# A filter's second layer on TensorE in quarter tiles, one step ahead, with one product moved from PSUM to SBUF

## Chip, core and metric

The kernel runs on one core of one Trainium2 chip. The metric is the device time of one execution in microseconds (us), the median of several runs. On the core, TensorE (PE in the profile, its weight loads PEld) multiplies matrices into PSUM; VectorE (DVE), ScalarE (ACT) and GpSimd (POOL) work element by element; SyncE (SP) issues most of the transfers. PSUM has eight banks of 512 float32 values in each of 128 partitions; SBUF is the large on-chip memory.

## The reference, cut to what matters

```python
def _attn_ref(x, v, pos_emb, w1, w2):            # x, v: 1 x 12480 x 128
    h_mlp = np.maximum(pos_emb @ w1, 0.0) @ w2   # filter: 64 features, second layer 64 -> 128
    h_filt = h_mlp * np.exp(-0.01 * pos)[:, None]
    Uf = np.fft.rfft(x * v, n=2 * S, axis=1)
    Hf = np.fft.rfft(h_filt, n=2 * S, axis=0)
    y = np.fft.irfft(Uf * Hf[None, :, :], n=2 * S, axis=1)[:, :S, :]
    return x * y
# then two mixture layers on the 12480 x 128 result:
#   g = relu(x @ w_in) ** 2;                x = g @ w_out
#   g = max(h, 0) + alpha * min(h, 0), h = x @ w_in2;   out = g @ w_out2
```

## The kernel before

The convolution is done with a Fourier transform of length 110 x 229, written as matrix products; it takes the first 313 us or so of the execution, the two dense layers the rest. The stages of the convolution follow each other: the filter's hidden layer (`z_stage`), its transform (`ar_stage`, `r_stage`), the signal's transform (`u_stage`), the product of both (`p_stage`), and the way back (`b_stage`, `y_stage`). The second layer of the filter, `w2`, is linear, so it is applied after the transform, inside `p_stage`: the transformed hidden layer lies in tiles `r` (three in SBUF, the others are fetched back from a spill in DRAM).

`p_stage(h, ...)` makes the product for one half h of the 128 channels, in 14 steps n (0 to 13 for h=0, 14 to 27 for h=1). A step covers 4 of the 56 frequencies of the length-110 transform. In each step:

- `filters(n, c)` (line 363) makes the filter's real (c=0) and imaginary (c=1) part on TensorE: four matmuls of 128 rows, 115 columns of weights and 128 moving columns for each c. The 128 rows are two frequencies of 64 features, and `w2_sb` is a block-diagonal matrix, half of it zeros, that keeps the two apart. Each goes to one of the two banks of `r_h`. A float32 matmul shows as two rows in the trace, so a step has 16 such rows.
- VectorE multiplies the signal's transform with each part (line 386): `T` gets one product, and the second goes to `wide`, a PSUM tile of two banks, or in the steps listed in `on_pool` to a second `T` tile in SBUF. In half 0 each product is two instructions (16 and 112 channels), in half 1 one.
- Two sums of 512 elements (line 396) turn the products into a complex one: on VectorE, from `T` and `wide`, or on GpSimd in the steps in `on_pool`.
- `finish` (line 357) adds and subtracts pairs of channels and writes the result over the signal's transform: on GpSimd, except in the very last step, where VectorE does it.

There are four `T` tiles, used in turn. What runs beside the two halves: half 0 runs together with `u_stage(1)`, the signal's transform for the other channels (lines 312 to 328 on TensorE, ScalarE and VectorE; lines 274 and 211 on GpSimd prepare its input); half 1 runs together with `b_stage(0)` (line 409 on TensorE, line 413 on ScalarE), which reads what half 0 has written. `b_stage(1)` reads what half 1 has written, so it starts when the last `finish` is done, and everything behind it follows. `run` takes turns between two generators, and each engine's queue is the order in which the program was written; nothing reorders it.

Names in the rows: `bank` and `pair` are PSUM banks, `G` and `R` hold the transforms of the two halves (and other things at other times), `w_sb` is the second layer's matrix, `w_buf` and `s_w`, `f_w`, `m_w` are buffers for decoding the dense layers' weights, which lie idle during `p_stage`.

```python
            for c, op in ((0, ALU.subtract), (1, ALU.add)):
                eng = nc.gpsimd if apart else nc.vector
                eng.tensor_tensor(out=A[:, :, c], in0=A[:, :, c], in1=B[:, :, 1 - c], op=op)
            finish(n, j, A)
```

Of the kernel before, what the change touches and what calls it, by code (L numbers as in the profile page):

```python
# [9 lines left out]
F32 = mybir.dt.float32  # L10
# [11 lines left out]
KA = HA + 1  # L22
# [36 lines left out]
def kernel(  # L59
# [18 lines left out]
    idft_o: bass.AP,  # L78
    out: bass.AP,
# [10 lines left out]
    six = [psum.tile([128, 512], F32, name=f"bank{i}") for i in range(6)]  # L90
    s_pair = ctx.enter_context(ExitStack())

    def last_two(name, *sizes):
        s_pair.close()
        pool = s_pair.enter_context(tc.tile_pool(name=name, bufs=1, space=PSUM))
        return [pool.tile([128, n], F32, name=f"{name}{i}") for i, n in enumerate(sizes)]

    banks = six + last_two("pair", 512, 512)
    r_any, r_six, r_a, r_b, r_h = Ring(banks), Ring(six), Ring(banks[0:2]), Ring(banks[2:5]), Ring(banks[5:8])
# [61 lines left out]
    def load_first(pool):  # L161
# [13 lines left out]
        nc.sync.dma_start(out=sig_sb, in_=sign)  # L175
        nc.sync.dma_start(out=dfa, in_=dft_a)
        load(3)
# [35 lines left out]
    def ar_stage():  # L213
# [7 lines left out]
        for c in range(F // 4):  # L221
            f0 = 4 * c
            p = [bank(r_six, HB, 4, K2) for s in range(2)]
            for s in range(2):
                for j in range(4):
                    nc.tensor.matmul(p[s][:, j], lhsT=rv[:, f0 + j, s], rhs=dfa[:, s * K2:(s + 1) * K2])  # L226
# [118 lines left out]
    on_pool = {2, 6, 10, 15, 18, 21, 24}  # L345

    def p_stage(h, t_ring, r_ring):
# [20 lines left out]
        first = []  # L368
        if h:
            first += [filters(nj, c) for c in range(2)]  # L370
            yield
        for n in range(h * nj, (h + 1) * nj):
# [7 lines left out]
            B = t_ring() if apart else wide[:HB].rearrange("p (x c k) -> p x c k", k=4, c=2)  # L380
            A = t_ring()
            for c, out_c in enumerate((A, B)):
                H = first.pop(0) if first else filters(n, c)
                hv = H.rearrange("p d s q r -> p (d s) (q r)")
                for x0, m in parts(h):
# [3 lines left out]
                        in1=hv[:, x0:x0 + m].unsqueeze(2).to_broadcast([HB, m, 2, 4]),  # L389
# [108 lines left out]
    def split_w(s, f, m, t, hi, lo, tail):  # L498
        words = s.rearrange("p t k -> p (t k)").bitcast(I32).rearrange("p (n w) -> p w n", w=2)
# [30 lines left out]
    def weights(pool, n=2):  # L530
        s_ring = ring_of(pool, 3, [128, n, 128], I64, "s_w")
        rings = [ring_of(pool, 2, [128, n * 128], F32, t) for t in ("f_w", "m_w")] + [Ring([])]

        def go(todo):
# [217 lines left out]
    with tc.manual_schedule():  # L752
        wst = ctx.enter_context(tc.tile_pool(name="wst", bufs=1))
        decode = weights(wst)
# [8 lines left out]
        with ExitStack() as st:  # L763
            late = st.enter_context(tc.tile_pool(name="late", bufs=1, side="right"))
            w2_sb = late.tile([128, 2 * D], F32, name="w2_sb")
# [18 lines left out]
            (wide,) = last_two("wide", 1024)  # L784
            r_b.items, r_h.items, r_ab.items = six[2:4], six[4:6], six[0:4]
# [98 lines left out]
def _tables(cell):  # L884
# [9 lines left out]
    ic[0] *= 0.5  # L894
    dft_b = np.zeros((HB, 3, HX), f)
# [8 lines left out]
    return w[cell].astype(f), dft_a, dft_b, e.astype(f), np.stack([o, -o], 1).astype(f)  # L904
# [59 lines left out]
```

## Time and profile before

| what | before |
|---|---|
| median of 3 runs | 1384.12 us (1383.98 to 1384.48) |
| profiled execution, its own time | 1384.36 us |
| span of the profiled execution | 1382.6 us |
| busy: TensorE, VectorE, ScalarE, GpSimd | 1374.7, 1146.6, 984.4, 1029.3 us |
| granted TensorE clock, mean | 1.00 |

The profiled execution's own time is its span and 1.8 us around it. The share of TensorE over the whole span says little on one stage: the product stage lies between about 118 and 243 us, and there three engines have nearly the same load. So the rows are read by stretch: 118 to 195.1 us is half 0 of the product, 195.1 to 243.3 us half 1. A timeline row merges instructions of one kind that follow each other: start, length in us, engine, line, operation, tiles, shapes and count, and in brackets the idle time of the engine before it with what ended it. Matmul ends are modelled, so the distance from start to start is read, not the length.

### The profile page before, as it was taken

To read this page: it belongs to the slowest core of one execution; us is meant where nothing else is said; L and a number is where in the kernel's file an instruction comes from. 1 tells how busy PE (TensorE), PEld (TensorE's weight loads), DVE (VectorE), ACT (ScalarE), POOL (GpSimd) and SP (SyncE) were. 2 spreads that over 40 slices of the span, in tenths; PEclk is the share of its full clock that TensorE was granted. 3 is DMA by queue.
4 is the path that set the end of the run, shared out by engine and by line. 5 is a ranking of instruction groups with operands and counts; after the bars stand their busy time and mean duration, and the time that the engine had idled before them with its cause. 6 is when DMAs were issued, how large, how long until landed. Compare 5 with 4: busy or idle time off the path is not lost.

```text
span 1382.6 us, 23568 instructions
## 1 busy us (share of the span) xinstructions
PE 1374.7 (99%) x8036; PEld 1193.9 (86%) x8036; DVE 1146.6 (83%) x1806; ACT 984.4 (71%) x1863; POOL 1029.3 (74%) x857
## 2 busy tenths in 40 slices
PE   9999999999999999999999999999999999999998
PEld 9999999998888888888888888888888888888898
DVE  6888989867888888888888878888888878888888
ACT  4453333638887777877777787778777787778777
POOL 4955969577877777777777777777777777777777
PEclk9999999999999999999999999999999999999999
DMA  8666423574000000000000000000000000000000
GB/s 250 185 199 186 129 65 114 157 245 146 31 2 0 9 9 1 8 9 8 9 9 9 8 1 9 9 8 8 9 8 1 9 8 8 9 9 9 1 8 19
DMA packets 59020, 66.27 MB, mean 48 GB/s; under 512 B 6226, under 2 KB 48019, under 8 KB 58771
## 3 DMA queue, kind: packets, MB, share of 16 engines
q1 hardware_dynamic: 58490, 64.56, 15.2%
q8 instruction: 63, 1.03, 0.3%
q14 instruction: 58, 0.48, 0.1%
q10 hardware_dynamic: 409, 0.21, 0.1%
HBM read 47.83 MB, written 16.92 MB: 47 GB/s over the span
## 4 chain that ended last, share of the span: by engine, by line
PE 96%; DVE 2%; issue 1%; POOL 1%; ACT 0%; POOLq 0%; DVEq 0%; ACTq 0%
PE bank L637 19%; PE bank L638 19%; PE bank L639 19%; PE pair L638 6%; PE pair L639 6%; PE pair L637 6%; PE bank L409 3%; PE bank L466 3%; PE bank L363 3%; PE bank L286 2%; PE bank L226 2%; PE bank L312 2%; PE bank L299 1%; PE pair L245 1%; PE bank L191 1%
## 5 line engine op out<-in xcount | busy, mean ns | idle before, releaser
L690 POOL TENSOR_TENSOR g<-R,g 128x512 fp32r<-128x512 f32 (+1 forms) x601 | 779.6, 1314 | 257.9 <-ACT g L679 243.7
L672 DVE SCALAR_TENSOR_TENSOR R<-bank,e 128x512 f32<-128x512 f32 (+1 forms) x800 | 530.8, 674 | 137.0 <-POOL g L690 99.2
L679 ACT CAST g<-R 128x512 fp32r<-128x512 f32 (+1 forms) x800 | 469.6, 605 | 76.6 <-DVE R L672 69.2
L657 ACT ACTIVATE e<-bank 128x512 f32<-128x512 f32 (+1 forms) x400 | 234.9, 587 | 104.0 <-PE bank L639 101.3
L662 DVE TENSOR_SCALAR e<-bank,alpha 128x512 f32<-128x512 f32 (+1 forms) x266 | 195.2, 734 | 35.9 <-PE bank L639 34.6
L690 DVE TENSOR_TENSOR g<-R,g 128x512 fp32r<-128x512 f32 (+1 forms) x199 | 185.0, 930 | 0.0
L638 PE MATMUL pair<-g,w_o 128*128 128x512 f32 (+1 forms) x400 | 153.7, 384 | 0.4 <-POOL g L690 0.4
L637 PE MATMUL bank<-x,w_i 128*128 128x512 f32 (+1 forms) x400 | 153.8, 385 | 0.0
L637 PE MATMUL pair<-g,w_o 128*128 128x512 f32 (+1 forms) x400 | 153.7, 384 | 0.0
L638 PE MATMUL bank<-x,w_i 128*128 128x512 f32 (+1 forms) x400 | 153.6, 384 | 0.0
L639 PE MATMUL bank<-x,w_i 128*128 128x512 f32 (+1 forms) x400 | 153.5, 384 | 0.0
L639 PE MATMUL pair<-g,w_o 128*128 128x512 f32 (+1 forms) x400 | 153.5, 384 | 0.0
L637 PE MATMUL bank<-g,w_o0b 128*128 128x512 f32 (+1 forms) x350 | 134.4, 384 | 0.0
L638 PE MATMUL bank<-g,w_o0b 128*128 128x512 f32 (+1 forms) x350 | 134.4, 384 | 0.0
L639 PE MATMUL bank<-g,w_o0b 128*128 128x512 f32 (+1 forms) x350 | 134.3, 384 | 0.0
L659 ACT ACTIVATE e<-bank 128x512 f32<-128x512 f32 (+1 forms) x134 | 78.8, 588 | 34.1 <-PE bank L639 32.5
L660 ACT ACTIVATE e<-e,alpha 128x512 f32<-128x512 f32 (+1 forms) x134 | 95.5, 713 | 4.4
L637 PEld LDWEIGHTS bank<-x,w_i 128*128 128x128 f32 x400 | 75.1, 188 | 15.0 <-DVE R L672 0.9
L638 PEld LDWEIGHTS pair<-g,w_o 128*128 128x128 f32 x400 | 75.1, 188 | 14.7 <-POOL g L690 1.0
L639 PEld LDWEIGHTS bank<-x,w_i 128*128 128x128 f32 x400 | 75.1, 188 | 14.4
L639 PEld LDWEIGHTS pair<-g,w_o 128*128 128x128 f32 x400 | 75.1, 188 | 14.4
L638 PEld LDWEIGHTS bank<-x,w_i 128*128 128x128 f32 x400 | 75.3, 188 | 13.8
(138 smaller groups left out, 2531.9 us busy)
## 6 DMA issues: line engine op xcount, KB each, us to landing
r<-spill SPq DMA_DIRECT2D x22, 460.0 KB, 3.3
G<-in_xs_dram SPq DMA_DIRECT2D x32, 224.0 KB, 3.8
G<-in_vs_dram SPq DMA_DIRECT2D x32, 224.0 KB, 3.7
spill<-r SPq DMA_DIRECT2D x14, 460.0 KB, 3.0
out_dram<-R SPq DMA_DIRECT2D x23, 256.0 KB, 2.0
s_w<-in_moe_w_out_dram SPq DMA_DIRECT2D x16, 256.0 KB, 5.3
s_w<-in_moe_w_in_dram SPq DMA_DIRECT2D x16, 256.0 KB, 2.9
w_spill<-w_o SPq DMA_DIRECT2D x15, 256.0 KB, 4.2
```

Of the source, the lines that this page charges most:

```text
L363: nc.tensor.matmul(H[:, :, s, q], lhsT=r_t[p_order[n]][:, q, 2 * s + c], rhs=w2_sb[:, h * D:(h + 1) * D])
L409: nc.tensor.matmul(p[:, d], lhsT=U(h, 2 * (x0 + d) + e, 1)[:, 0], rhs=icosb if e == 0 else isinb)
L637: nc.tensor.matmul(p, lhsT=wl, rhs=xh, start=first, stop=False)
L638: nc.tensor.matmul(p, lhsT=wh, rhs=xl, start=False, stop=False)
L639: nc.tensor.matmul(p, lhsT=wh, rhs=xh, start=False, stop=last)
L657: nc.scalar.activation(out=r, in_=p, func=ACTF.Relu)
L659: nc.scalar.activation(out=r, in_=p, func=ACTF.Relu, scale=-1.0)
L660: nc.scalar.activation(out=r, in_=r, func=ACTF.Copy, scale=alpha[:, t:t + 1])
L662: nc.vector.tensor_scalar(out=r, in0=p, scalar1=0.0, scalar2=alpha[:, t:t + 1], op0=ALU.min, op1=ALU.mult)
L672: nc.vector.scalar_tensor_tensor(out=g, in0=p, scalar=0.0, in1=r, op0=ALU.max, op1=op)
L679: nc.scalar.copy(out=gh, in_=g)
L690: eng.tensor_tensor(out=gl, in0=g, in1=gh.bitcast(F32), op=ALU.subtract)
```

## The change

- `filters(n)` now makes both parts in one call, with 32 matmuls in place of 8. Each takes 64 rows (one frequency), 64 or 51 columns of weights, and 64 moving columns, so it uses one quarter of the array; the four quarters (two row groups, two column groups) come in turn. The two row groups write to different banks. `w2_sb` holds the 64 x 128 matrix twice, one below the other, without zeros.
- It writes to one of two places of two banks each (`filt`, named wide0 and wide1 in the rows), in turn; so all eight banks are the four `bank` tiles and these two places. The filter of step n+1 is written in the program ahead of the products of step n.
- The second product goes to `wide` in SBUF, which is now a part of `w_buf`, the buffer for decoding weights, so the sums on VectorE read both operands from SBUF.
- `on_pool` has nine steps: 2, 5, 8, 11 in half 0 and 15, 17, 19, 22, 25 in half 1 (before 2, 6, 10 and 15, 18, 21, 24).
- The order of the frequencies in the filter's transform is changed by another table, `dff`, which is loaded ahead of `dfa`; the sizes of that stage's matmuls stay.

```diff
-    six = [psum.tile([128, 512], F32, name=f"bank{i}") for i in range(6)]
+    four = [psum.tile([128, 512], F32, name=f"bank{i}") for i in range(4)]
...
-    on_pool = {2, 6, 10, 15, 18, 21, 24}
+    on_pool = {2, 5, 8, 11, 15, 17, 19, 22, 25}
...
-        def filters(n, c):
-            H = bank(r_h, HB, DH, 2, 2, 2)
+        def filters(n):
+            k, w = n // nj * DH, r_t[p_order[n]]
+            H = filt[n % 2].rearrange("p (r q c d s) -> p r q c d s", r=2, q=2, c=2, s=2)
             for q in range(2):
                 for s in range(2):
-                    nc.tensor.matmul(
-                        H[:, :, s, q], lhsT=r_t[p_order[n]][:, q, 2 * s + c], rhs=w2_sb[:, h * D:(h + 1) * D]
-                    )
-            return H
...
+                    for c in range(2):
+                        for r in range(2):
+                            f = slice(F * r, F * r + F)
+                            for b in (slice(0, 64), slice(64, HB)):
+                                nc.tensor.matmul(H[b, r, q, c, :, s], lhsT=w[f, q, 2 * s + c, b], rhs=w2_sb[f, k:k + DH])
...
+        if not h:
+            filters(0)
         for n in range(h * nj, (h + 1) * nj):
...
-            B = t_ring() if apart else wide[:HB].rearrange("p (x c k) -> p x c k", k=4, c=2)
+            if n + 1 < 2 * nj:
+                filters(n + 1)
+            hv = filt[n % 2][:HB].rearrange("p (k c x) -> p c x k", k=4, c=2)
+            B = t_ring() if apart else wide
             A = t_ring()
             for c, out_c in enumerate((A, B)):
-                H = first.pop(0) if first else filters(n, c)
-                hv = H.rearrange("p d s q r -> p (d s) (q r)")
                 for x0, m in parts(h):
                     nc.vector.tensor_tensor(
                         out=out_c[:, x0:x0 + m],
                         in0=at_j(x0, m, j),
-                        in1=hv[:, x0:x0 + m].unsqueeze(2).to_broadcast([HB, m, 2, 4]),
+                        in1=hv[:, c, x0:x0 + m].unsqueeze(2).to_broadcast([HB, m, 2, 4]),
                         op=ALU.mult,
                     )
...
-        decode = weights(wst)
+        w_buf = wst.tile([128, 10 * 256], F32, name="w_buf")
+        wide = w_buf[:HB, 1536:2560].rearrange("p (x c k) -> p x c k", k=4, c=2)
+        decode = weights(w_buf)
...
-            (wide,) = last_two("wide", 1024)
+            filt = last_four("wide", 1024, 1024)
```

TensorE's queue, one step of half 0 before (line 363 is the filter, 312 and 320 to 325 are the signal's transform; a row is one matmul instruction, with its output's size and the count):

```order
L363 MATMUL bank_73<-w_sb,r_111 115x64x2 x4
L312 MATMUL bank_69<-dfa,G 115x112 x4
L312 MATMUL bank_70<-dfa,G 115x112 x4
L363 MATMUL bank_74<-w_sb,r_111 115x64x2 x4
L320 MATMUL bank_72<-G,dfb 115x4x56
L321 MATMUL bank_71<-G,dfb 115x4x56
L322 MATMUL bank_72<-G,dfb 115x4x56
L325 MATMUL bank_71<-G,dfb 115x4x56
```

The same now (line 370 is the filter, of which 28 more rows like the first two are left out):

```order
L370 MATMUL wide_1129<-w_sb,r_105 64x64
L370 MATMUL wide_1129<-w_sb,r_105 51x64
...
L314 MATMUL bank_69<-dfa,G 115x112 x4
L314 MATMUL bank_70<-dfa,G 115x112 x4
L322 MATMUL bank_72<-G,dfb 115x4x56
L323 MATMUL bank_71<-G,dfb 115x4x56
L324 MATMUL bank_72<-G,dfb 115x4x56
L327 MATMUL bank_71<-G,dfb 115x4x56
```

Two blocks of four matmuls became one block of 32 smaller ones, ahead of the step's other work; the other rows stay.

VectorE's queue, the first four steps of half 1 before (386 products, 396 sums):

```order
L386 TENSOR_TENSOR T_1137<-R_82,bank_73 115x1024
L386 TENSOR_TENSOR wide_1132<-R_82,bank_74 115x1024
L396 TENSOR_TENSOR T_1137<-T_1137,wide_1132 115x128x4 x2
L386 TENSOR_TENSOR T_1139<-R_82,bank_73 115x1024
L386 TENSOR_TENSOR T_1138<-R_82,bank_74 115x1024
L386 TENSOR_TENSOR T_1136<-R_82,bank_73 115x1024
L386 TENSOR_TENSOR wide_1132<-R_82,bank_74 115x1024
L396 TENSOR_TENSOR T_1136<-T_1136,wide_1132 115x128x4 x2
L386 TENSOR_TENSOR T_1137<-R_82,bank_73 115x1024
L386 TENSOR_TENSOR wide_1132<-R_82,bank_74 115x1024
L396 TENSOR_TENSOR T_1137<-T_1137,wide_1132 115x128x4 x2
```

And now (389 products, 399 sums; `w_buf` is the SBUF buffer, `wide` the filter's place in PSUM):

```order
L389 TENSOR_TENSOR T_1135<-R_82,wide_1128 115x1024
L389 TENSOR_TENSOR w_buf<-R_82,wide_1128 115x1024
L399 TENSOR_TENSOR T_1135<-T_1135,w_buf 115x128x4 x2
L389 TENSOR_TENSOR T_1133<-R_82,wide_1129 115x1024
L389 TENSOR_TENSOR T_1136<-R_82,wide_1129 115x1024
L389 TENSOR_TENSOR T_1134<-R_82,wide_1128 115x1024
L389 TENSOR_TENSOR w_buf<-R_82,wide_1128 115x1024
L399 TENSOR_TENSOR T_1134<-T_1134,w_buf 115x128x4 x2
L389 TENSOR_TENSOR T_1136<-R_82,wide_1129 115x1024
L389 TENSOR_TENSOR T_1135<-R_82,wide_1129 115x1024
```

The sums that stay on VectorE take `T` and `w_buf` in place of `T` and a PSUM tile, and the fourth step's sums (step 17) have left the queue.

GpSimd's queue in half 1 before (357 is `finish`, 396 the sums):

```order
L357 TENSOR_TENSOR R_82<-T_1137 115x64x2x4 x2
L396 TENSOR_TENSOR T_1139<-T_1139,T_1138 115x128x4 x2
L357 TENSOR_TENSOR R_82<-T_1139 115x64x2x4 x2
L357 TENSOR_TENSOR R_82<-T_1136 115x64x2x4 x2
L357 TENSOR_TENSOR R_82<-T_1137 115x64x2x4 x2
L396 TENSOR_TENSOR T_1139<-T_1139,T_1138 115x128x4 x2
```

And now (359 and 399):

```order
L359 TENSOR_TENSOR R_82<-T_1135 115x64x2x4 x2
L399 TENSOR_TENSOR T_1133<-T_1133,T_1136 115x128x4 x2
L359 TENSOR_TENSOR R_82<-T_1133 115x64x2x4 x2
L359 TENSOR_TENSOR R_82<-T_1134 115x64x2x4 x2
L399 TENSOR_TENSOR T_1136<-T_1136,T_1135 115x128x4 x2
L359 TENSOR_TENSOR R_82<-T_1136 115x64x2x4 x2
```

The second pair of sums comes one `finish` earlier; over half 1 there are five pairs for four.

## Rows read from the trace of the kernel before

**Rows 1.** The page: the chain that ended last, shares of the span by engine.

```profile
PE 96%; DVE 2%; issue 1%; POOL 1%; ACT 0%; POOLq 0%; DVEq 0%; ACTq 0%
```

**Rows 2.** Busy us by stretch: length, PE, PEld, DVE, ACT, POOL, clock, DMA share, GB/s.

```profile
118.00:195.10 77.10, 76.64 (x627) 74.87 (x625) 66.69 (x110) 25.07 (x47) 61.98 (x76) 1.00 0.41 123
195.10:243.30 48.20, 47.08 (x451) 46.73 (x449) 45.92 (x50) 17.27 (x32) 42.05 (x34) 1.00 0.38 113
```

**Rows 3.** Timeline of TensorE, one step of half 0.

```profile
161.96 1.04 PE L363 MATMUL bank<-w_sb,r 128*115 128x128 f32 x8
162.84 1.77 PE L312 MATMUL bank<-dfa,G 110*115 110x112 f32 x16
164.45 1.04 PE L363 MATMUL bank<-w_sb,r 128*115 128x128 f32 x8
...
166.84 1.04 PE L363 MATMUL bank<-w_sb,r 128*115 128x128 f32 x8
```

**Rows 4.** Timeline of TensorE, one step of half 1.

```profile
227.07 1.91 PE L363 MATMUL bank<-w_sb,r 128*115 128x128 f32 x16
...
228.81 1.75 PE L409 MATMUL bank<-dfb,G 115*112 115x116 f32 x16
...
230.40 1.91 PE L363 MATMUL bank<-w_sb,r 128*115 128x128 f32 x16
```

**Rows 5.** Timeline of GpSimd in half 1.

```profile
198.92 2.50 POOL L357 TENSOR_TENSOR R<-T 115x512 f32<-115x512 f32 x2 [8.22 <-DVE T L396]
201.35 2.53 POOL L396 TENSOR_TENSOR T<-T,T 115x512 f32<-115x512 f32 x2
...
233.93 7.45 POOL L357 TENSOR_TENSOR R<-T 115x512 f32<-115x512 f32 x6
```

**Rows 6.** Timeline of GpSimd in half 0: first and last `finish`.

```profile
124.54 2.78 POOL L357 TENSOR_TENSOR G<-T 115x64 f32<-115x64 f32 x4 [10.91 <-DVE T L396]
...
187.93 2.77 POOL L357 TENSOR_TENSOR G<-T 115x64 f32<-115x64 f32 x4 [2.13 <-DVE T L396]
```

**Rows 7.** Groups of VectorE in half 1: count, busy us, mean ns, idle before.

```profile
L386 DVE TENSOR_TENSOR T<-R,bank 115x1024 f32<-115x1024 f32 x18 | 21.6, 1216 | 1.9 <-PE bank L363 1.8
L396 DVE TENSOR_TENSOR T<-T,wide 115x512 f32<-115x512 f32 x20 | 12.9, 684 | 0.3
```

**Rows 8.** Timelines of VectorE and TensorE where half 1 ends.

```profile
242.45 1.29 DVE L357 TENSOR_TENSOR R<-T 115x512 f32<-115x512 f32 x2
...
243.29 2.90 PE L409 MATMUL bank<-dfb,R 115*112 115x116 f32 x27 [1.12 <-DVE R L357]
```

**Rows 9.** Dense layers, line 690: group on GpSimd, durations on VectorE, one meeting.

```profile
L690 POOL TENSOR_TENSOR g<-R,g 128x512 fp32r<-128x512 f32 (+1 forms) x601 | 779.6, 1314 | 257.9 <-ACT g L679 243.7
...
L690 DVE TENSOR_TENSOR g<-R,g x199: 512/683/1811, 317.2 to 1378.0; 128x512 fp32r<-128x512 f32 x185, 128x352 fp32r<-128x352 f32 x14
...
403.69 1.65 DVE L690 TENSOR_TENSOR g<-R,g 128x512 fp32r<-128x512 f32 x1
...
403.49 3.00 POOL L690 TENSOR_TENSOR g<-R,g 128x512 fp32r<-128x512 f32 x2 [0.44 <-ACT g L679]
```

**Rows 10.** Timeline of TensorE in `y_stage`, two column groups in turn, and its end.

```profile
312.93 0.43 PE L466 MATMUL bank<-ide,G 112*64 112x110 f32 x4
313.12 0.43 PE L466 MATMUL bank<-ido,G 112*64 112x110 f32 x4
313.48 0.50 PE L637 MATMUL bank<-xa,w_i 128*128 128x512 f32 x1
```

**Rows 11.** Timeline of TensorE where `y_stage` begins.

```profile
269.25 0.72 PE L445 MATMUL bank<-w_i 128*128 128x112 f32 x5
269.90 0.33 PE L466 MATMUL bank<-ide,G 112*64 112x55 f32 x4
```

**Rows 12.** Timeline of VectorE: the first products of half 0 and half 1.

```profile
119.13 1.28 DVE L386 TENSOR_TENSOR T<-G,bank 115x128 f32<-115x128 f32 x2 [1.26 <-PE bank L363]
...
195.16 1.22 DVE L386 TENSOR_TENSOR T<-R,bank 115x1024 f32<-115x1024 f32 x1
```

More of the change, by code (lines that the diff above doesn't have):

```diff
@@ L89, with last_four @@
     psum = ctx.enter_context(tc.tile_pool(name="psum", bufs=1, space=PSUM))
[L90 to L95 removed]
+    four = [psum.tile([128, 512], F32, name=f"bank{i}") for i in range(4)]
+    s_four = ctx.enter_context(ExitStack())
+    def last_four(name, *sizes):
+        s_four.close()
+        pool = s_four.enter_context(tc.tile_pool(name=name, bufs=1, space=PSUM))
         return [pool.tile([128, n], F32, name=f"{name}{i}") for i, n in enumerate(sizes)]
[L98 to L99 removed]
+    banks = four + last_four("lone", 512, 512, 512, 512)
+    r_any, r_six, r_a, r_b, r_h = Ring(banks), Ring(banks[:6]), Ring(banks[0:2]), Ring(banks[2:5]), Ring(banks[5:8])
     r_ab, r_y = Ring([]), Ring([])
@@ L175, in load_first @@
         nc.sync.dma_start(out=sig_sb, in_=sign)
+        nc.sync.dma_start(out=dff, in_=dft_f)
+        load(3)
         nc.sync.dma_start(out=dfa, in_=dft_a)
-        load(3)
         nc.sync.dma_start(out=dfb, in_=dft_b)
@@ L225, in ar_stage @@
                 for j in range(4):
-                    nc.tensor.matmul(p[s][:, j], lhsT=rv[:, f0 + j, s], rhs=dfa[:, s * K2:(s + 1) * K2])
+                    nc.tensor.matmul(p[s][:, j], lhsT=rv[:, f0 + j, s], rhs=dff[:, s])
             for s, copy in enumerate((nc.scalar.copy, nc.vector.tensor_copy)):
@@ L528, with weights @@
     STEPS = 7
-    def weights(pool, n=2):
-        s_ring = ring_of(pool, 3, [128, n, 128], I64, "s_w")
-        rings = [ring_of(pool, 2, [128, n * 128], F32, t) for t in ("f_w", "m_w")] + [Ring([])]
+    def weights(buf, n=2):
+        m = n * 128
+        s_ring = Ring(buf[:, 2 * m * i:2 * m * (i + 1)] for i in range(3))
+        rings = [Ring(buf[:, m * i:m * (i + 1)] for i in (j, j + 1)) for j in (6, 8)] + [Ring([])]
         def go(todo):
@@ L543, in load @@
                     tiles[i] = [s_ring()]
-                    nc.sync.dma_start(out=tiles[i][0], in_=parts[i][0])
+                    nc.sync.dma_start(
+                    out=tiles[i][0].bitcast(I32).rearrange("p (t k) -> p t k", t=n), in_=parts[i][0].bitcast(I32)
+                )
             def size(i):
@@ L764 @@
             late = st.enter_context(tc.tile_pool(name="late", bufs=1, side="right"))
-            w2_sb = late.tile([128, 2 * D], F32, name="w2_sb")
+            w2_sb = late.tile([128, D], F32, name="w2_sb")
             dfa = late.tile([NA, 2 * K2 + KA], F32, name="dfa")
@@ L769 @@
             with tc.tile_pool(name="early", bufs=1) as early:
+                dff = early.tile([NA, 2, K2], F32, name="dff")
                 run((z_stage(*load_first(early)), 1))
@@ L789 @@
             u = u_stage(1)
-            run((some(u, 2 * NG - 1), 2 * NG), (p0, 2 * nj + 3))
-            next(q0)
+            run((some(u, 2 * NG - 1), 2 * NG), (p0, 2 * nj + 2))
             next(u)
             next(back)
-            run((b_stage(0, False), NG), (q0, 2 * nj + 3))
-        banks = six + last_two("pair", 512, 512)
-        r_y.items = six
+            run((b_stage(0, False), NG), (q0, 2 * nj + 2))
+        banks = four + last_four("apart", 512, 512, 512, 512)
+        r_y.items = banks[:6]
         wa = ctx.enter_context(tc.tile_pool(name="wa", bufs=1))
```

23 lines of the change are left out of this document (10 added, 13 removed).

## The prediction

> **What bounds the kernel now.** Read the page first: the chain that ended last is 96% TensorE [rows 1], so a stage is only worth reading where another engine could take TensorE's place. The change touches the product stage, 118 to 243.3 us, so the second view is the busy time of that stretch by half [rows 2]. In half 0 TensorE is busy 76.6 of 77.1 us, VectorE 66.7, GpSimd 62.0; in half 1 TensorE 47.1 of 48.2, VectorE 45.9, GpSimd 42.1. Three engines are nearly level, at a granted clock of 1.00 throughout.
>
> The timelines say the same by step. A step of half 0 is 4.88 us from filter to filter (161.96 to 166.84), in which TensorE's rows follow each other without a gap; the filter takes 0.88 us twice, 1.76 in all [rows 3]. A step of half 1 is 3.33 us: 1.74 for the filter and 1.59 for `b_stage` [rows 4]. GpSimd in half 1 does not rest at all from 198.92 to 241.38: 13 `finish` pairs of 2.49 us (7.45 for three) and four pairs of sums of 2.52 [rows 5]. In half 0 it starts at 124.54 and ends at 190.70, and near the end waits at least 2.13 us for VectorE, so it has a little slack there [rows 6]. What follows starts when VectorE's own `finish` ends, at 243.74; TensorE waited 1.12 us for it [rows 8]. So in half 1 the chain can change hands at once: an engine that gets 1 us more work there is late by about 1 us.
>
> **The filter on TensorE.** Removed: 16 trace rows of 109 ns (1.74 us over 16) in each of 28 steps. Added: 32 matmuls, 64 rows. The nearest rows are those of `y_stage`, which uses two column groups of 64 in turn [rows 10]: four rows in 0.19 us, 47.5 ns a row, where rows of 112 and 116 moving columns on the whole array take 100 ns (1.61 us for 16) [rows 3, 4]. So two quarters do overlap. A float32 matmul is two passes on the same quarter, the second behind the first, and issue is in order; so the second pass of one matmul can run beside the first pass of the next, and no third. That makes one matmul cost one pass: 0.095 us in `y_stage`. A pass of 64 columns is half of the 109 ns of 128 columns, 54.5 ns; 32 of them are 1.74 us. The block costs what it did: half the array's work, but only two of the four quarters at a time.
>
> To that come two changes between whole array and quarters in each step. Where `y_stage` begins, its first row starts 0.65 us after the first of five rows, which take 0.11 us each, so 0.1 late [rows 11]; where it ends 0.36 us pass from the first of its last four rows, which take 0.19, to the next kind: 0.17 us [rows 10]. Both places also wait for other engines, so 0.27 us is an upper bound and 0 the lower; I take 0.25, since both rows show a delay. Over 14 steps of half 0 that is +3.5 us, with rounding **+4 us** at the end of half 0, where TensorE is the bound. Bounds of the block: 0.87 us if four quarters ran at once, 3.49 (32 x 109 ns) if nothing overlapped.
>
> The Trainium skill ("TensorEngine Tiling (Array Packing)", section Key Properties) says that different tiles can load and multiply in parallel. By that rule a block would be the 0.87 us above; the rows show two at a time, and no row here has four.
>
> **The step ahead.** VectorE waited for the filter 1.8 us in half 1 [rows 7]. That goes, but VectorE isn't what is late there, so it is worth 0 to 1.8; I take 0. The larger load of `dff`, the other order of loads, and the staging buffer's sharing with the decode lie beside work that doesn't wait for them; 0.
>
> **Sums from SBUF.** Before, a sum on VectorE read `T` and a PSUM tile, and took 684 ns while GpSimd was busy beside it [rows 7]. Now both operands are in SBUF. The kernel has such an instruction elsewhere: line 690 in the dense layers, 512 elements, both in SBUF. Alone it takes 683 ns, but up to 1811 [rows 9]. One meeting shows why: it starts 0.20 us after a GpSimd instruction, and takes 1.65 us; the two GpSimd instructions at that place take 3.00 us together, where one takes 1.31 in the mean. VectorE stood until GpSimd's instruction ended, and GpSimd's next stood until VectorE was done. So they exclude each other: VectorE lost 0.97 us (1.65 less 0.68), GpSimd 0.4 (3.00 less 2.6).
>
> GpSimd is nearly always at work during the product, so nearly every sum meets one. A pair of sums: the first waits for what is left of an instruction, on average half of 1.25 us, less the 0.1 that the row shows to be hidden, so 0.5; the second waits for the whole of the next one, 1.0. That is 1.5 us a pair for VectorE and 0.8 for GpSimd. Behind a waiting sum on VectorE stand the next step's products, and in half 0 the sums of line 328, which free TensorE's banks; `finish` on GpSimd waits for it too. Steps with sums on VectorE: 10 in half 0 and 9 in half 1. The first of each half runs before GpSimd has work, and the last about when it is done: 9 and 7 pairs meet.
>
> **Nine sums on GpSimd.** One pair more in each half: GpSimd +2.5 us each, VectorE -1.3 each.
>
> **The sum.** Half 0: TensorE ends 4 us later, so half 1's first product starts at 199.2 in place of 195.16 [rows 12]. GpSimd has 62.0 + 2.5 + 9 x 0.8 = 71.7 us from 124.5, so it ends at 196.2, before that; VectorE has 66.7 - 1.3 + 9 x 1.5 = 78.9 of 81 us, just inside. Half 1: GpSimd starts at 198.9 + 4 = 202.9 and has 42.05 + 2.5 + 7 x 0.8 = 50.2 us, to 253.1. VectorE has 45.9 - 1.3 + 7 x 1.5 = 55.1 us from 199.2 and 0.7 us of gaps, to **255.0**. TensorE has 14 x (1.59 + 1.99) = 50.1, to 249.3. The last of them, VectorE, ends 11.3 us behind the 243.74 of before. Nothing behind changes. The profiled execution took 1384.36 us (span 1382.6), 0.24 over the median: **1395.7 us**.
>
> **Rivals.** (1) Four quarters run at once, and the sums still exclude. TensorE then ends half 0 some 12 us (14 x 0.87) earlier, but VectorE's work doesn't shrink: 66.7 + 45.9 - 2.6 + 24 = 134 us, from its start at 119.1 [rows 12] to 253.1, 9.4 us later than before: about 1393. For it speaks the rule above, against it the pace of [rows 10]. Chance 0.14.
>
> (2) The quarters don't overlap, or a pass takes twice as long. Then a block is 3.49 us and a step 0.25 more: half 0 gets 14 x 2.0 = 28 us longer, half 1 the same, since TensorE outlasts the others: 1384.4 + 56 = 1440. For it: each output element now stands alone, 8 bytes from the next, where the old filter wrote pairs; no row shows that. Against it: the pace in [rows 10]. Chance 0.09. The Trainium skill ("PSUM — Partial Sum Buffer", section Specifications (TRN2)) says that any non-contiguous access pattern slows matmuls, with lines of 8 bytes; the filter of before, with pairs 32 bytes apart, kept 109 ns for 128 columns, so for pairs the trace doesn't agree.
>
> (3) **Faster.** The sums hardly meet, because GpSimd and VectorE fall into step, and four quarters run at once. Then GpSimd alone is the limit: 104.0 + 5.1 = 109.1 us from about 123.5, to 232.6, 8.8 us ahead of its 241.4: 1375.6. It decides from the point where fewer than about 10 of the 16 pairs meet, with TensorE's block under 1.5 us. Against it: GpSimd has no gap in which a sum could run [rows 5]. Chance 0.09.
>
> (4) Both costs are small (0.05 us a change of shape, half of the meetings): VectorE 134 - 12 is 122 us, which TensorE hides again, and the end moves by 1 to 2 us: 1386. Chance 0.08.
>
> **How the numbers follow.** My forecast, both costs as summed, has 0.60; with its bounds (a shape change of 0 to 0.27 us, a pair of sums costing 1.0 to 2.2 us) it reaches from 1389 to 1405, and a little over where TensorE waits for VectorE's banks in half 0 too. The range, 1385.5 to 1409, holds it, rival 1 and most of 4, and leaves out 2 and 3. A measurement tells 0.2%, 2.8 us, from no change. Slower: forecast, rivals 1 and 2, 0.83. Same: 0.08. Faster: 0.09.
>
> **What would show it.** In the new profile the line of the sums on VectorE (399) should have a median well over 0.684 us and a maximum over 1.6; GpSimd's lines 359 and 399 should have instructions stretched by 0.3 us or more; a block of line 370 should take 1.7 to 1.8 us from first to last start, with two rows starting together. `b_stage(1)` on line 412 should begin near 254 us. A block near 0.9 us is rival 1, near 3.5 rival 2; sums that stay at 0.68 us would make the prediction wrong at its main term.

## The result, and the profile after

The changed kernel takes **1402.1 us** (median; 1401.1 to 1403.0) against 1384.3 for the kernel before: ratio 1.0128, 95% interval 1.0111 to 1.0146, so 17.8 us slower. The forecast was 1395.7, the range 1385.5 to 1409. The profiled execution took 1401.19 us (span 1399.4; before 1384.36 and 1382.6), 16.8 us more.

In the page's chain of waits TensorE's share has fallen from 96% [rows 1] to 91%:

```profile
PE 91%; DVE 6%; POOL 2%; issue 1%; ACT 0%; POOLq 0%; ACTq 0%; DVEq 0%
```

Busy time by stage: from the first product of half 0 to the first of half 1, from there to VectorE's end, and from there to `y_stage` (columns: length, busy us of PE, its weight loads, DVE, ACT, POOL, with counts; then granted clock, DMA share, GB/s). It answers to [rows 2]:

```profile
119.80:201.70 81.90, 69.20 (x1279) 62.59 (x1272) 72.10 (x109) 24.51 (x46) 69.00 (x78) 1.00 0.36 113
201.70:258.70 57.00, 44.32 (x1077) 41.41 (x1077) 56.55 (x48) 17.38 (x32) 49.81 (x36) 0.94 0.36 107
258.70:286.60 27.90, 27.90 (x267) 27.84 (x265) 21.82 (x53) 21.74 (x52) 14.60 (x20) 0.94 0.31 99
```

TensorE, which before had gaps of 0.5 us in half 0 and 1.1 in half 1 [rows 2], is now idle 12.7 us in each. In half 1 VectorE has taken its place, 56.55 of 57.00 us busy; in half 0 no engine is full. The sums on VectorE and on GpSimd (min/median/max in ns):

```profile
L399 DVE TENSOR_TENSOR T<-T,w_buf x38: 676/1001/2860, 122.3 to 255.7; 115x512 f32<-115x512 f32 x38
L399 POOL TENSOR_TENSOR T<-T,T x18: 1264/1274/1737, 135.3 to 249.3; 115x512 f32<-115x512 f32 x18
```

One place in half 1, VectorE and then GpSimd (start, length of the merged run, count), answering to [rows 5]; the first line is a pair of sums on VectorE before:

```profile
241.13 1.29 DVE L396 TENSOR_TENSOR T<-T,wide 115x512 f32<-115x512 f32 x2
...
224.38 3.51 DVE L399 TENSOR_TENSOR T<-T,w_buf 115x512 f32<-115x512 f32 x2
...
224.37 2.97 POOL L399 TENSOR_TENSOR T<-T,T 115x512 f32<-115x512 f32 x2
227.42 5.68 POOL L359 TENSOR_TENSOR R<-T 115x512 f32<-115x512 f32 x4
```

GpSimd starts 0.01 us ahead of VectorE. A pair of sums took 1.29 us on VectorE before; here 3.51. GpSimd's own pair takes 2.97 for 2.52 [rows 5], and four `finish` instructions take 5.68 where six took 7.45, so four 4.97. Each engine's instruction stands while the other's runs. Of the 19 pairs on VectorE, five meet no GpSimd instruction and last 1.29 to 1.31 us, as before; the other 14, six in half 0 and eight in half 1, last 1.48 to 3.59.

TensorE's filter block in both halves, answering to [rows 3, 4]:

```profile
160.39 1.16 PE L370 MATMUL wide<-w_sb,r 64*64 64x64 f32 x64 [1.06 <-DVE w_buf L389]
161.48 0.64 PE L322 MATMUL bank<-G,dfb 115*115 115x224 f32 x2
...
201.65 1.16 PE L370 MATMUL wide<-w_sb,r 64*64 64x64 f32 x64
202.73 1.84 PE L412 MATMUL bank<-dfb,G 115*112 115x116 f32 x16
204.50 1.15 PE L370 MATMUL wide<-w_sb,r 64*64 64x64 f32 x64
```

64 rows take 1.09 us from start to the next kind's start, 17 ns a row over the block; `b_stage`'s 16 rows behind them 1.77 for 1.59 [rows 4], so the changes of shape cost about 0.18 there. Within the block the trace has each quarter's rows 56 to 58 ns behind each other, in all four quarters at once: 16 rows at 57 ns are 0.91 of the 1.09 us. At the end of half 1, VectorE and TensorE, answering to [rows 8]:

```profile
255.06 2.35 DVE L399 TENSOR_TENSOR T<-T,w_buf 115x512 f32<-115x512 f32 x2
257.45 1.29 DVE L359 TENSOR_TENSOR R<-T 115x512 f32<-115x512 f32 x2
...
258.29 4.96 PE L412 MATMUL bank<-dfb,R 115*112 115x116 f32 x31 [2.68 <-DVE R L359]
```

Behind that, one more thing is new. TensorE's granted clock in steps of 2 us:

```profile
256.00:258.00 2.00, 0.00 (x0) 0.00 (x0) 1.97 (x2) 0.19 (x1) 0.86 (x1) 1.00 0.03 10
258.00:260.00 2.00, 1.72 (x15) 1.75 (x16) 0.74 (x2) 0.55 (x1) 0.00 (x0) 0.91 0.00 0
260.00:262.00 2.00, 2.00 (x13) 2.00 (x12) 0.65 (x2) 0.85 (x2) 0.00 (x0) 0.50 0.00 0
262.00:264.00 2.00, 2.00 (x17) 2.00 (x17) 1.86 (x6) 1.24 (x4) 0.72 (x1) 0.73 0.00 0
264.00:266.00 2.00, 2.00 (x23) 2.00 (x22) 1.67 (x4) 1.87 (x5) 0.84 (x3) 1.00 0.39 131
```

After 2.68 us without a matmul the clock falls to 0.50, the 1.2 GHz level, for some 3.4 us: 13 rows in 2 us where 23 fit at 1.00. Before, it stayed at 1.00. In half 1 of the changed kernel the clock had fallen twice already, at about 235.8 us (at the end of a gap of 2.83 us) and at about 249.4 (behind one of 1.73), each time for some 3.4 us; there VectorE sets the pace.

The stages of the profiled executions, from the timelines (us from the span's start: first product of each half, end of VectorE's last `finish`, first row of `y_stage`):

| kernel | first of half 0 | first of half 1 | VectorE's end | `y_stage` | median, us |
|---|---|---|---|---|---|
| before | 119.13 | 195.16 | 243.74 | 269.90 | 1384.3 |
| after | 119.81 | 201.66 | 258.74 | 286.56 | 1402.1 |
| e1 product in SBUF | 119.74 | 204.42 | 260.96 | 290.16 | 1400.7 |
| e2 nine sums | 119.88 | 195.87 | 245.40 | 271.37 | 1385.7 |
| e4 seven sums | 119.63 | 202.71 | 259.24 | 287.27 | 1403.1 |
| e5 sums read own place | 119.51 | 206.50 | 254.69 | 283.20 | 1398.8 |
| e10 sums read other place | 120.14 | 197.21 | 245.37 | 274.05 | 1388.1 |
| e13 whole-array filter | 119.12 | 201.59 | 258.78 | 286.60 | 1401.2 |
| e3 one place, product in PSUM | 118.95 | 204.38 | 277.73 | 303.89 | 1412.4 |
| e7 filter repeated | 118.89 | 202.38 | 259.61 | 288.39 | 1402.4 |
| e8 two banks as one tile | 128.38 | 217.04 | 265.36 | 306.10 | 1637.9 |
| e9 rows by quarter | 121.87 | 232.56 | 301.23 | 327.45 | 1442.7 |
| e11 filler rows | 119.87 | 202.92 | 260.18 | 286.33 | 1400.7 |
| e12 tiles in half 1 | 119.18 | 196.11 | 244.43 | 274.52 | 1388.1 |

The profiled executions lie within 1.3 us of these medians, but for e1's (1404.5 us, 3.8 above) and e3's (1418.3, 5.9 above).

So the 16.7 us from before to after up to `y_stage` are: 0.7 at the start, 5.8 in half 0 (81.85 for 76.03), 8.5 in half 1 (57.08 for 48.58), 1.7 behind it (27.82 for 26.16). From there on the two differ by 0.1 us.

### The profile page after: what moved, and what is told of

Its sections match the earlier page's. It is cut to its first block, busy times and chain, and to the rows that moved or that the text cites. A ratio compares the mean times of both kernels' runs of the same rounds, so it can differ in the third digit from the quotient of the medians.

```text
span 1399.4 us, 26222 instructions
## 1 busy us (share of the span) xinstructions
PE 1367.3 (98%) x9380; PEld 1179.1 (84%) x9380; DVE 1161.5 (83%) x1802; ACT 984.9 (70%) x1863; POOL 1044.4 (75%) x861
## 4 chain that ended last, share of the span: by engine, by line
PE 91%; DVE 6%; POOL 2%; issue 1%; ACT 0%; POOLq 0%; ACTq 0%; DVEq 0%
PE bank L643 13%; PE bank L645 13%; PE bank L644 13%; PE apart L643 12%; PE apart L644 12%; PE apart L645 12%; PE bank L469 2%; PE bank L288 2%; PE lone L247 2%; DVE T L399 2%; DVE T L389 2%; PE bank L412 1%; DVE w_buf L389 1%; PE bank L228 1%; PE bank L301 1%
## 5 line engine op out<-in xcount | busy, mean ns | idle before, releaser
L644 PE MATMUL apart<-g,w_o 128*128 128x512 f32 (+1 forms) x400 | 153.7, 384 | 0.4 <-POOL g L696 0.4
L643 PE MATMUL apart<-g,w_o 128*128 128x512 f32 (+1 forms) x400 | 153.6, 384 | 0.0
L645 PE MATMUL apart<-g,w_o 128*128 128x512 f32 (+1 forms) x400 | 153.5, 384 | 0.0
L643 PE MATMUL apart<-g,w_o0b 128*128 128x512 f32 (+1 forms) x350 | 134.4, 384 | 0.0
L645 PE MATMUL apart<-g,w_o0b 128*128 128x512 f32 (+1 forms) x350 | 134.3, 384 | 0.0
L644 PE MATMUL apart<-g,w_o0b 128*128 128x512 f32 (+1 forms) x350 | 134.3, 384 | 0.0
L644 PEld LDWEIGHTS apart<-g,w_o 128*128 128x128 f32 x400 | 75.1, 188 | 14.7 <-POOL g L696 1.0
L645 PEld LDWEIGHTS apart<-g,w_o 128*128 128x128 f32 x400 | 75.1, 188 | 14.4
```

The source lines that it names most:

```text
L643: nc.tensor.matmul(p, lhsT=wl, rhs=xh, start=first, stop=False)
L644: nc.tensor.matmul(p, lhsT=wh, rhs=xl, start=False, stop=False)
L645: nc.tensor.matmul(p, lhsT=wh, rhs=xh, start=False, stop=last)
```

## The experiments

### Is it the product in SBUF, or the nine sums? (e1, e2, e4)

e1 puts one part of the change into the kernel before:

```diff
-            B = t_ring() if apart else wide[:HB].rearrange("p (x c k) -> p x c k", k=4, c=2)
+            B = t_ring() if apart else wide
...
+        wide = w_buf[:HB, 1536:2560].rearrange("p (x c k) -> p x c k", k=4, c=2)
```

> The kernel before with one part of the change alone: the imaginary product lies in the staging buffer in SBUF in place of two PSUM banks (the banks stay unused); filter on the whole array, seven GpSimd sums as before. Theory (VectorE's sums with both operands in SBUF and GpSimd's instructions exclude each other): sums on VectorE go from a mean of 0.68 us to 1.1 or more, maximum over 1.6; 21 pairs at 1.5 to 3 us of delay, of which half 0 hides part: 1400 to 1412 us. Rival (the loss is GpSimd's two more sums, or TensorE's small tiles): within 3 us of before, 1383 to 1387.

Measured: 1400.7 us, ratio 1.0125 (1.011 to 1.014). This part alone costs 16.2 us, which can't be told from the whole change's 17.8. VectorE's sums, and GpSimd's `finish`, which no line of the edit touches, before (last line) and in e1:

```profile
L396 DVE TENSOR_TENSOR T<-T,w_buf x42: 677/804/4107, 123.6 to 259.0; 115x512 f32<-115x512 f32 x42
...
L357 POOL TENSOR_TENSOR R<-T 115x512 f32<-115x512 f32 x26 | 35.8, 1403 | 12.9 <-DVE T L396 12.5
...
L357 POOL TENSOR_TENSOR R<-T 115x512 f32<-115x512 f32 x26 | 32.2, 1268 | 8.6 <-DVE T L396 8.2
```

e2 puts nine sums on GpSimd in the kernel before (shown); e4 takes the changed kernel back to seven, the same two lines the other way:

```diff
-    on_pool = {2, 6, 10, 15, 18, 21, 24}
+    on_pool = {2, 5, 8, 11, 15, 17, 19, 22, 25}
```

> The kernel before with another part of the change alone: nine sums on GpSimd in place of seven; second product in PSUM and filter on the whole array as before. Theory (exclusion is the cause; GpSimd has 2 us of room in half 1): sums on VectorE stay at 0.68 us, time 1383 to 1388 us. Rival (GpSimd's load is the cause): GpSimd's work of half 1 ends 2.5 to 5 us later and with it the stage, 1387 to 1392.

> The changed kernel with the seven GpSimd sums of before in place of nine. Theory (exclusion): two more pairs on VectorE, each 1.3 us of its own and 1 to 2 us of waiting, less what GpSimd loses: 1403 to 1409 us, slower than the changed kernel. Rival (GpSimd's load is the cause): 2.5 us a half come back, 1396 to 1400.

Measured: e2 1385.7, ratio 1.0009 (1.0000 to 1.0019), within what the theory said; e4 1403.1, ratio 1.0136 (1.0121 to 1.0151), which can't be told from the change's 1.0128. e4 lies at the lower edge of what theory said and above all that the rival said. So the number of GpSimd sums matters little either way. In e2 the sums keep their 684 ns, but the last `finish` on VectorE, which has both operands in SBUF in every kernel here, now meets GpSimd and takes 2.50 us for 1.29:

```profile
L396 DVE TENSOR_TENSOR T<-T,wide x38: 678/684/690, 123.8 to 242.2; 115x512 f32<-115x512 f32 x38
...
242.90 2.50 DVE L357 TENSOR_TENSOR R<-T 115x512 f32<-115x512 f32 x2
```

### The changed kernel without the meeting (e5, e10)

Both change only which memory the second operand of VectorE's sums is read from: a PSUM place of the filter, so that one operand stays in SBUF. The sums then add other numbers, and nobody reads the product in `w_buf`; instructions, sizes and order stay. Shown is e5; e10 has `filt[(n + 1) % 2]` in the same place.

```diff
-                eng.tensor_tensor(out=A[:, :, c], in0=A[:, :, c], in1=B[:, :, 1 - c], op=op)
+                in1 = B[:, :, 1 - c]
+                if not apart:
+                    in1 = filt[n % 2][:HB].rearrange("p (x c k) -> p x c k", k=4, c=2)[:, :, 1 - c]
+                eng.tensor_tensor(out=A[:, :, c], in0=A[:, :, c], in1=in1, op=op)
```

> The changed kernel, in which VectorE's sums read as their second operand the filter's PSUM place of the same step in place of the product in SBUF (that part of the computation is changed: the sums add other numbers); the instructions, their sizes and their order stay. Theory (exclusion): the sums fall back to 0.68 us, GpSimd's instructions to 1.25, and with the cheap filter the stage is bounded by VectorE and GpSimd at about 110 us: 1372 to 1380 us. Rival (the loss comes from GpSimd's two more sums, from the step ahead or from TensorE's tiles): 1396 to 1402 as the changed kernel.

> As the run in which VectorE's sums read the filter's PSUM place of their own step (other numbers are added, so that part of the computation is changed), but here they read the place of the next step, which is written long before and whose next writer waits for a later product anyway: no place is held longer than in the changed kernel. Theory (the exclusion on SBUF is the whole loss): sums at 0.68 us, no wait put in its stead, 1374 to 1382 us. Rival (part of the loss of half 0 is a chain that the order makes, the filter's block on TensorE waiting for the last product of the step before and the other stage's matmuls standing behind it): half 0 stays at 78 to 82 us from first to first product, half 1 falls to 45 to 48: 1386 to 1394.

e5: 1398.8 us, ratio 1.0108 (1.0093 to 1.0124): the rival's number, and a blow to the theory if only the time is read. But its sums took 678 ns and its half 1 48.2 us, 8.9 less than after; half 0 had become 87.0 us. There VectorE waits, and TensorE's block waits for the sums, because they hold the place that the next block is to write (half 0: busy time; waits: total, times, longest):

```profile
119.50:206.50 87.00, 72.14 (x1277) 65.22 (x1268) 63.57 (x108) 24.50 (x46) 64.64 (x78) 0.96 0.34 106
...
DVE R L330 <- ACT G L326: 20.0, 10, 3.4
...
PE wide L370 <- DVE T L402: 11.2, 8, 2.3
```

e10 reads the other place, which no writer wants at that time: 1388.1 us, ratio 1.0026 (1.0015 to 1.0038). That is in the rival's range, not in the theory's 1374 to 1382. The first row is the sums' duration, the next two are the two halves, the last the `finish` on VectorE:

```profile
L402 DVE TENSOR_TENSOR T<-T,wide x38: 676/678/681, 122.5 to 242.0; 115x512 f32<-115x512 f32 x38
...
120.10:197.20 77.10, 68.82 (x1279) 62.66 (x1269) 63.49 (x108) 24.48 (x46) 64.47 (x78) 1.00 0.38 120
197.20:245.40 48.20, 41.32 (x1078) 38.49 (x1078) 45.66 (x48) 17.35 (x32) 44.17 (x36) 1.00 0.41 127
...
242.75 2.62 DVE L359 TENSOR_TENSOR R<-T 115x512 f32<-115x512 f32 x2
```

Without the meeting of sums and GpSimd 14.0 of the 17.8 us come back (1402.1 - 1388.1): in the profiles 4.8 in half 0 and 8.9 in half 1. GpSimd's busy time falls with it, from 69.00 and 49.81 to 64.47 and 44.17. So the exclusion holds both ways and is most of the loss. Against before, e10 keeps 1.0 us at the start, 1.0 in half 0 and 2.5 behind the products, less 0.4 in half 1. The 2.5 come with its last `finish`, which meets GpSimd (2.62 us for 1.29): TensorE is idle for 3.09 us and then for 0.61 more, and its clock falls to 0.50. The rival is right in its own part: half 0 stays at 77 us, just under the 78 to 82 it said, although no engine is busy for more than 69 of it. VectorE waits there 13.5 us for ScalarE's copies (line 330 for line 326), against 4.9 before.

The Trainium skill ("SBUF — State Buffer", section Who interferes with whom) has the rule: a VectorE instruction with two SBUF inputs contends with a GpSimd instruction that reads SBUF, and one with at most one SBUF input, outside VectorE's two-port modes, does not. These runs agree: 676 to 681 ns with one in e10, up to 2860 with two in the changed kernel.

### TensorE's block (e13, e9)

e13 is the changed kernel with the whole-array filter (and the old table for the filter's transform), in the same four banks and a step ahead:

```diff
-                                nc.tensor.matmul(H[b, r, q, c, :, s], lhsT=w[f, q, 2 * s + c, b], rhs=w2_sb[f, k:k + DH])
+                    nc.tensor.matmul(
+                        H[:, :, s, q], lhsT=r_t[p_order[n]][:, q, 2 * s + c], rhs=w2_sb[:, g * D:(g + 1) * D]
+                    )
```

> The changed kernel with its filter put back on the whole array: 16 matmul rows of 109 ns a step less the tiles' block, in the same four banks, as a step ahead as there, product in the staging buffer, nine GpSimd sums. Theory (TensorE is not what holds the changed kernel, so its cheaper block changes nothing): 1400 to 1404 us. Rival (the tiles' 0.5 us a step count): 1406 to 1412.

Measured: 1401.2 us, ratio 1.0121 (1.0108 to 1.0135), as the theory said. TensorE has 9 us more to do in half 0 and 5.7 in half 1, and no stage is longer by more than 0.7 us:

```profile
119.10:201.60 82.50, 78.22 (x617) 74.00 (x616) 71.94 (x109) 24.51 (x46) 68.89 (x78) 1.00 0.37 114
201.60:258.80 57.20, 49.98 (x453) 48.89 (x452) 56.71 (x48) 17.35 (x32) 49.31 (x36) 0.97 0.33 105
```

e9 issues the 32 matmuls by quarter:

```diff
-            for q in range(2):
-                for s in range(2):
-                    for c in range(2):
-                        for r in range(2):
-                            f = slice(F * r, F * r + F)
-                            for b in (slice(0, 64), slice(64, HB)):
+            for r in range(2):
+                f = slice(F * r, F * r + F)
+                for b in (slice(0, 64), slice(64, HB)):
+                    for q in range(2):
+                        for s in range(2):
+                            for c in range(2):
```

> The changed kernel with the filter's 32 matmuls in another order: the eight of one quarter of the array behind each other, then the next quarter's. Theory (a row of 64 columns keeps its own quarter busy for about 55 ns, half of the 109 ns of 128 columns, and four quarters work at once only if rows for other quarters follow each other): a block takes about 64 x 55 ns = 3.5 us in place of 1.1, TensorE becomes the bound in both halves: 1430 to 1445 us. Rival (the order does not matter, rows wait for something else): 1.1 us a block, 1401 to 1403.

Measured: 1442.7 us, ratio 1.0424 (1.0408 to 1.0439). The block:

```profile
232.56 3.32 PE L370 MATMUL wide<-w_sb,r 64*64 64x64 f32 x64
235.80 1.84 PE L412 MATMUL bank<-dfb,G 115*112 115x116 f32 x16
```

3.24 us, 51 ns a row over the block, near the 3.5 us expected, against 17 when rows for four quarters alternate. Row by row, a quarter takes its rows 56 to 58 ns behind each other in both kernels, each with its own load of weights; the average in e9 is a little lower because the first rows for the next quarter start before the last ones of the quarter before. So the pace of a quarter is the same, in the changed kernel all four go at it at once, and the order of issue is worth a factor of 3.

### The clock behind the products (e7, e11)

> The changed kernel, in which half 1's filter writes half of its outputs twice (16 more matmuls a step, same values), so that TensorE, which idles 12.7 us there, idles less. Theory (some 1.7 us of the loss is TensorE's granted clock, which fell to its lower level behind such idle time): the granted clock of the stretch from 228 to 264 us stays nearer to 1.00 and the stage behind the products is up to 1.7 us shorter: 1400 to 1401.5 us. Rival (the clock costs nothing, or its loss has another cause than idle time): 1402 or more.

In half 1 the filter writes half of its outputs a second time:

```diff
-                    for c in range(2):
+                    for c in [0, 1, 0, 1][:2 if n < nj or q else 4]:
```

Measured: 1402.4 us, ratio 1.0130 (1.0115 to 1.0145), no difference from after and the rival's number. It tells nothing of the clock's price, since the added rows end with the last filter: the gap ahead of `b_stage(1)` stays (3.96 us here) and the clock falls there as in after.

```profile
256.00:258.00 2.00, 0.00 (x0) 0.00 (x0) 2.00 (x2) 0.00 (x0) 1.13 (x1) 0.93 0.34 131
258.00:260.00 2.00, 0.84 (x4) 0.88 (x5) 1.57 (x3) 0.00 (x0) 0.00 (x0) 0.50 0.00 0
```

e11 puts rows into that gap:

```diff
             run((b_stage(0, False), NG), (q0, 2 * nj + 2))
+            for _ in range(14):
+                nc.tensor.matmul(filt[0][:HB, :HX], lhsT=cosb, rhs=icosb)
```

> The changed kernel with 14 extra matmuls (28 rows of about 0.1 us) on TensorE behind the last matmul of the first inverse stage, into a dead PSUM place, so that TensorE is not idle in the 2.7 us ahead of the second inverse stage. Theory (the granted clock falls to its lower level because of that idle time, and the slow rows of 258 to 264 us cost 1.2 to 1.7 us): the clock stays at 1.00 there and the time is 1400.4 to 1401.2 us, the span from the stage's first to y_stage's first row near before's 26.6 us. Rival (the clock falls all the same, or the copies behind hold the stage): 1402 to 1404.

Measured: 1400.7 us (1399.4 to 1401.2), ratio 1.0115 (1.0101 to 1.0129). The intervals of e11 and after overlap, so the time alone, which is the theory's, doesn't decide; the rows do. The gap is 1.61 us and the clock stays:

```profile
259.72 3.40 PE L412 MATMUL bank<-dfb,R 115*112 115x116 f32 x32 [1.61 <-DVE R L359]
...
260.00:262.00 2.00, 2.00 (x23) 2.00 (x22) 0.18 (x1) 0.97 (x2) 0.00 (x0) 1.00 0.00 0
262.00:264.00 2.00, 2.00 (x23) 2.00 (x22) 1.44 (x4) 0.53 (x3) 0.00 (x0) 1.00 0.00 0
```

From VectorE's end to `y_stage` it is 26.15 us, as before (26.16), where after has 27.82. That is the 1.7 us, and it is what 3.4 us at half the clock are worth.

### Tiles without the SBUF sums (e3, e8, e12)

Three tries for a version that beats both; none does. e3 and e8 give the filter one place of two banks, so that the product can go back to PSUM:

```diff
-            filt = last_four("wide", 1024, 1024)
+            place, wide = last_four("wide", 1024, 1024)
```

> The changed kernel with three parts undone: the second product is back in two PSUM banks, so the filter has one place of two banks and is issued by halves of 16 matmuls just ahead of each product, as before; seven sums on GpSimd. Left of the change: the 64 x 64 tiles. Theory (a block of 64 rows takes 1.1 us and the two changes of shape in a step about 0.2 each): a step of half 0 is 0.2 to 0.4 us shorter, half 1 is then held by VectorE's 45.9 us: 1377 to 1382 us. Rival (the tiles gain nothing, or TensorE waits for VectorE to free the one place): 1384 to 1392.

> Second product in PSUM as before, 64 x 64 tiles in one block of 32 matmuls a step; in half 0 one place, in half 1, where two banks of the other stage are given to it, two places and the filter a step ahead; three sums on GpSimd in half 0, five in half 1. Theory: half 0 gains 14 steps of about 0.45 us, half 1 falls to what VectorE and GpSimd need, 44.6 us for 48.2: 1373 to 1378 us. Rival (the one place in half 0 makes TensorE wait for VectorE, the two banks of the inverse stage hold it up in half 1): 1382 to 1390.

e3: 1412.4 us, ratio 1.0207 (1.0177 to 1.0236), with sums at 684 ns: slower still than the rival's 1384 to 1392. With one place, TensorE and VectorE take turns (waits of e3's half 1):

```profile
PE wide L369 <- DVE T L389: 18.8, 13, 1.8
DVE T L389 <- PE wide L369: 17.0, 10, 3.3
```

e8: 1637.9 us, ratio 1.184. Its half 1, with two places and five sums, takes 44.6 us from first to last product, less than the 45.9 before; its half 0, with one, 88.7 from first to first product. Of its loss 217 us lie behind the first row of `y_stage` and are a slip of the experiment: two banks became halves of one tile, which the dense layers then treat as one and wait for (one of the waits for it, dense layers):

```profile
PE half L648 <- DVE R L683: 81.4, 97, 2.2
```

e12 keeps half 0 as before and makes half 1 as in e8, with tiles of their own for the banks:

```diff
+            *pl, wide_r[0] = last_four("wide", 1024, 1024, 1024)
+            filt += pl
```

> Half 0 as before: whole-array filter, second product in PSUM, three GpSimd sums. Half 1 with 64 x 64 tiles, two places and a step ahead, the second product in PSUM all the same (two banks are taken from the inverse stage, which keeps two), five GpSimd sums. Theory (without sums that have both operands in SBUF, the tiles and the step ahead take VectorE's wait for the filter away): half 1 from first to last product 44 to 45 us for 45.9, 1381.5 to 1383.5 us. Rival (two banks hold the inverse stage up, or GpSimd with five sums ends last): 1384 to 1388.

Measured: 1388.1 us, ratio 1.0025 (1.0015 to 1.0035), above the theory's 1381.5 to 1383.5 and at the upper edge of the rival's range, though for another cause. From `y_stage` to the end it takes as long as before, so e8's 217 us are gone with the shared tile. The products of half 1 take 44.6 us, as forecast, but the last `finish` on VectorE meets GpSimd (2.35 us for 1.29), TensorE idles 2.89 us, and its clock falls for longer than in after:

```profile
243.94 1.05 PE L419 MATMUL bank<-dfb,R 115*112 115x116 f32 x8 [2.89 <-POOL R L359]
...
246.00:248.00 2.00, 2.00 (x12) 2.00 (x12) 0.00 (x0) 0.47 (x2) 0.00 (x0) 0.50 0.00 0
248.00:250.00 2.00, 2.00 (x13) 2.00 (x12) 1.49 (x4) 0.52 (x3) 0.00 (x0) 0.50 0.00 0
250.00:252.00 2.00, 2.00 (x13) 2.00 (x12) 1.86 (x6) 1.48 (x4) 1.46 (x2) 0.52 0.06 12
```

From VectorE's end to `y_stage` 30.09 us pass, 3.9 more than before. Another place for that `finish`, or filler rows as in e11, wasn't tried.

## Why the prediction was right, and where not

The sign, the main mechanism and the stretch were right; the time was 6.4 us short, and two of its steps were wrong in a way that the total hides. Of the 6.4 us, in the profiles, 0.7 came at the start, 1.8 in half 0, 1.3 in half 1 and 1.7 behind it; the other 0.9 is that the profiled execution lies below the median.

**The sums from SBUF** (its main term): right. From one meeting in the dense layers [rows 9] it made 1.5 us a pair for VectorE and 0.8 for GpSimd, with 16 pairs meeting. Measured against e10, VectorE's sums are 20.0 us busier (44.26 and 24.24 us), and GpSimd 10.2 us. Shared among the 14 pairs that meet, that is 1.4 us a pair for VectorE and 0.7 for GpSimd, so the price was near; two pairs fewer meet than forecast, six for 9 in half 0, where the sums cost 8.0 us for 13.5, and eight for 7 in half 1, where they cost 12.0 for 10.5. In half 1 VectorE's busy time was put at 55.1 us and is 56.55, and it sets the end there, as forecast; the stage takes 57.1 us for the 55.8 in the sum. The signs it named are there: median 1.001 us, maximum 2.86, GpSimd's sums up to 1.74 for 1.27. A wait can outlast one GpSimd instruction, which the prediction had not allowed: in the sum of 2.86 us, which starts at 172.12, it is 2.86 - 0.68 = 2.18 us: two GpSimd instructions of 1.28 us, the first begun 0.19 us ahead of it, run one behind the other while it stands. `b_stage(1)` began at 258.3 us, not near 254.

**The filter on TensorE**: wrong. The step that failed is that a float32 matmul's second pass lets only two quarters run at once. It took the 47.5 ns a row in `y_stage` [rows 10] as the most that order of issue allows; `y_stage` uses only two tiles, and in the trace each of them takes a row every 95 ns, beside the other. The changed kernel uses four, and each takes a row of 64 columns every 56 to 58 ns, beside the other three. The block is 1.09 us and the changes of shape 0.18 behind it, 1.27 in place of the 1.99 of the sum. The Trainium skill ("TensorEngine Tiling (Array Packing)", section Key Properties) says that different tiles can load and multiply in parallel, and was right against that reading: the block is near the 0.87 us that the prediction worked out for four at once. e13 shows that it didn't matter: with a block on the whole array the time is the same.

**Half 0**: +4 was forecast for TensorE's sake, +5.8 came, for another cause, so it is luck that the two lie near each other. TensorE was idle 12.7 us of it. e10 gives 4.8 to the exclusion; the other 1.0 stays in e10. The prediction had VectorE "just inside" with 78.9 us of work; it had 72.1 and yet held the stage up, because it isn't filled but sits in a loop: its last product frees the place, TensorE's block writes it, `u_stage`'s matmuls stand behind the block, ScalarE copies their result, and VectorE waits for the copy (line 330, 9.2 us in half 0 against 4.9 before). e5 shows that loop at work: a place held for the sums lengthens half 0 by 9.9 us against e10, with VectorE and GpSimd as busy as there. TensorE's rows took 3.3 us longer in it, at a granted clock of 0.96 for 1.00; how much of the 9.9 us that makes isn't known. How the 4.8 us divide over the waits is argued, not shown.

**The step ahead**, taken at 0, and **the nine sums**: with the tiles and both of these in it, e10's half 1 goes from 48.6 to 48.2 us; e2's time goes up by 1.3 us. Both are near the nothing or little that they were given. No run has the step ahead alone.

**What was missing**: 1.7 us of lower clock behind the products (e11 shows it), and 0.7 at the start, where the kernels, e8 and e9 left out, differ by up to 1.3 us without a cause that these runs tell.

**The rivals**: rival 1 had both mechanisms right, four quarters at once and the exclusion, and came to 1393. Of the mechanisms it gave the better account, though its number lies further off. Its step that failed is that VectorE would work without a gap from 119.1 us; it idles 9.8 us in half 0, in the loop above. Rival 2's price for rows that don't overlap, 1440, is what e9 made by order of issue, 1442.7. Rival 3 needed the sums to miss GpSimd; e10, in which no sum is lengthened by it, shows that even then the time is 1388 and not 1376, and without the 2.5 us behind the products it would still be some 1386.

## What to carry to other kernels

Before a tensor moves from PSUM to SBUF, look at which VectorE instructions get two SBUF operands by it, and whether GpSimd works at that time: here 38 sums of 0.68 us became 1.20 in the mean and GpSimd slowed as well; put alone into the kernel before, the move lost 16 us. An engine's busy share doesn't tell the cost of such a wait where it stands in a loop through other engines: compare a run in which only the operand's place differs. And a gap that opens on TensorE can cost again behind it, when its clock falls.

## What the hardware showed that was not expected

- 64 x 64 tiles in float32: 17 ns a row over a block when four quarters alternate, 51 ns when eight matmuls for one quarter follow each other (e9), with an output element every 8 bytes in both. Each quarter takes a row every 56 to 58 ns in both.
- A VectorE sum beside GpSimd can wait for longer than one GpSimd instruction of 1.27 us: sums of 0.68 us took up to 2.86 in the changed kernel and 4.11 in e1.
- TensorE's clock fell to 0.50 for about 3.4 us in the changed kernel after 2.68 us without a matmul, and for nearly 7 us in e12 after 2.89; after 1.61 us in e11 it stayed at 1.00, and so it did before after 1.12 [rows 8]. The length of the last gap alone doesn't tell: in the changed kernel the clock stayed at 1.00 behind a gap of 2.61 us in half 0 (176.6 to 179.2 us) and fell in half 1 behind one of 1.73.
